# Small edits to a tuned kernel: bias groups, load order, tile order, zero fill, reciprocals

## The chip, the cores and the metric

The kernel runs on one core of a Trainium2 chip. The metric is the device time of one execution in microseconds (us), lower is better. TensorE is called PE in the rows, with PEld for its weight loads; VectorE is DVE, ScalarE is ACT, GpSimd is POOL, and SP is the engine that issues most DMAs.

## The reference

Attention with a relative bias made by a small network, then a routed expert layer, then a gated output layer. Cut to what matters here:

```python
scores = scale * np.matmul(q, k.transpose(0, 1, 3, 2))       # 2 batches, 8 heads, 576 rows, 64 wide
x = (psi_rel / psi_i)[..., None]                             # log1p|i-j| over log1p(max(i,1))
bias = np.maximum(x @ w1 + b1, 0.0) @ w2                     # hidden 32, one value for each head
scores = scores + bias.transpose(2, 0, 1)[None]
attn = np.exp(scores - np.max(scores, axis=-1, keepdims=True))
attn = attn / (np.sum(attn, axis=-1, keepdims=True) + 1e-09)
out = np.matmul(attn, v)
# then: each row goes to one of 8 experts (dropped rows stay zero), then a SwiGLU layer to [1152, 512]
```

## The kernel before

The order of every engine's instructions is written out by hand; an engine runs its own list in order, and a wait holds everything behind it on that engine.

**The bias phase** (`bias_phase`) makes the bias of all heads. For each of 36 groups `k` of 16 query rows, `hidden(k)` makes four tiles `r` of 128x576 (line 554 on DVE: multiply by a per-row slope `sl`, then max; or line 552 on ACT as a Relu). The fourth tile of a group goes to ACT when `k % 5` is in `ONA`, that is in 21 of the 36 groups. Sixteen small matmuls (line 558) contract them into the PSUM tile `pb`, the ACT tile first; there are two such tiles, and 12 buffers for `r`. `leave(k)` adds a constant `kap` on ACT (line 567) and stores the group to DRAM (`biasd`, line 568). On ACT the order is `r` of group k, then `leave` of group k-1. `kap` is copied by DVE (lines 541 and 542) from `pk`, a product that PE makes behind its 14 warming matmuls. From group 20 on, ACT and DVE also split the first head's queries and keys into a high and a low part.

SP first issues loads of `wb`, `cst`, `ptab` and the two halves of the table `ltab`, in this order, and later the stores and, after the last group, the last bias tiles of head 0 (lines 189 to 193).

**The attention phase** (`attn_phase`) walks through 72 tiles, nine for a head: four of batch 0, one that holds the last 64 rows of both batches (`t == 4`), four of batch 1. Step `u` issues, in this order: loads for the next head on SP (`load`, line 220, at `u % 9` of 0 and 5; `bias` at 1 to 5), the scores of tile u+1 (line 279), the exponential of tile u-1 (line 311), the transposes of tile u-2 (lines 331 and 334), the maximum of tile u (`bound`, line 294), the low part of tile u-3 (`low`, line 350), and a share of the queued products with V (`pv`, line 378) and folds (`folds`, line 400). `folds(h)` takes the sums of head h, adds 1e-9 and takes the reciprocal on DVE (lines 392 and 393), and scales the result `xh` (line 403), whose PSUM bank is single. By the written shares it runs at step 9h + 17.

A loaded head is split by POOL (lines 231 to 242): for each of two batches, five steps on the raw tile, of which there are two buffers. The scores of the next head wait for them (`K2`, line 235). At step 12 one DMA fills the whole output with zeros (line 435).

After attention come routing, the experts and the output layer, which are not touched.

Of the kernel before, what the change touches and what calls it, by code (L numbers as in the profile page):

```python
# [8 lines left out]
F32 = mybir.dt.float32  # L9
# [4 lines left out]
AF = mybir.ActivationFunctionType  # L14
ALU = mybir.AluOpType
# [3 lines left out]
B, H, S, D, C = 2, 8, 576, 64, 32  # L19
N, DM, E, FF, F2 = B * S, H * D, 8, 1024, 1536  # L20
# [3 lines left out]
NT = 9  # L24
# [19 lines left out]
ENGINES = {getattr(mybir.EngineType, e) for e in ("DVE", "Pool", "Activation", "PE", "SP")}  # L44


ONA = (1, 3, 4)
L0, L1 = 20, 2
STEPS1 = 4

LOADS = (0, 5)
SHARE, SHARE4 = 0.68, 0.0
LAST = (2.0, 2.0, 2.0, 2.0)
LATE = ((7, 0, 1), (7, 1, 0), (7, 1, 1))
# [84 lines left out]
def view(t, off, *dims):  # L139

    base = t[:]
    return bass.AP(tensor=base.tensor, offset=base.offset + off, ap=[list(base.ap[0])] + [list(d) for d in dims])
# [105 lines left out]
def attn_phase(tc, ctx, load, cst, bias, zeros, fold, lg, x_p, rows, ps):  # L248
    nc = tc.nc
    V, A = nc.vector, nc.scalar  # L250
# [3 lines left out]
    m_p = ctx.enter_context(tc.tile_pool(name="am", bufs=4))  # L254
    ident = cst[:, C_ID:C_ID + 128]
    load, qk, loads = load
    bias, head = bias
    seq = []
    for h in range(H):
        seq += [(h, 0, t) for t in range(4)] + [(h, -1, 4)] + [(h, 1, t) for t in range(4)]  # L260
    mid = {}
    sco, ex, tp, tt, sums, pt, ot = {}, {}, {}, {}, {}, {}, {}

    def batches(u):
        h, b, t = seq[u]
# [100 lines left out]
    def pv(h, b, n):  # L366

        if h not in ot:
            ot[h] = o_p.tile([128, N], F32, name="ot")
        o = ot[h]  # L370
        hi, lo = pt[h, b]
        W = qk[h, b][3]
        a, w = ((0, 256), (256, 320))[n]
        po = bank((h, b, n) in LATE)
        k = 0
        for kt in range(5):
            for src in ((hi, lo) if kt < 4 else (hi,)):
                nc.tensor.matmul(po[:, :w], W[:, kt], src[:, kt, a:a + w], start=k == 0, stop=k == 8)  # L378
                k += 1
                if k < 9:  # L380
                    yield w / 2400
        A.activation(o[:, b * 512 + a:b * 512 + a + 256], po[:, :256], AF.Copy)
        if w > 256:
            A.activation(o[:, 1024 + b * 64:1088 + b * 64], po[:, 256:w], AF.Copy)
        if n:
            del pt[h, b]
        yield 0

    def folds(h):
        o = ot.pop(h)  # L390
        rs = m_p.tile([128, NT], F32, name="rs")
        V.tensor_scalar(rs, sums[h], 1e-9, None, op0=ALU.add)
        V.reciprocal(rs, rs)
        xh = x_p.tile([128, NT * RW], F32, name="xh").rearrange("p (t c) -> p t c", t=NT)
        w = fold[:, h // 2, h % 2 * E:h % 2 * E + RW]
        x, g = (xh[:, :, E:], xh[:, :, :E]) if h % 2 == 0 else (xh[:, :, :D], xh[:, :, D:])
        for t0, tn in ((0, 5), (5, 4)):
            pf = bank(h == H - 1)[:, :5 * RW].rearrange("p (t c) -> p t c", c=RW)
            for t in range(t0, t0 + tn):
                nc.tensor.matmul(pf[:, t - t0], o[:, t * 128:(t + 1) * 128], w, start=True, stop=True)  # L400
                if t < t0 + tn - 1:
                    yield 0.12
            V.tensor_tensor(xh[:, t0:t0 + tn], pf[:, :tn], view(rs, t0, (1, tn), (0, RW)), op=ALU.mult)
            if t0:
                nc.sync.dma_start(
                    rows.rearrange("(t p) d -> p t d", p=128)[:, :, h * D:(h + 1) * D], x
                )
                if h == 0:
                    nc.gpsimd.tensor_copy(lg, g)
                else:  # L410
                    (V if h == H - 1 else nc.gpsimd).tensor_tensor(lg, lg, g, op=ALU.add)
            yield 0
# [1 line left out]
    nu = len(seq)  # L414

    work = []
    for h in range(H):
        work += [(9 * h + 6, pv(h, 0, 0))] + ([(0, folds(h - 1))] if h else [])
        work += [(9 * h + 9, pv(h, 0, 1)), (9 * h + 11, pv(h, 1, 0)), (9 * h + 13, pv(h, 1, 1))]
    work.append((0, folds(H - 1)))  # L420
    share = 0.0
# [1 line left out]
    while work:  # L423
        u += 1
        if u < nu:
            h, b, t = seq[u]
            if h + 1 < H and u % 9 in LOADS:
                b = LOADS.index(u % 9)
                loads.append(load(h + 1, b))
                qk[h + 1, b] = next(loads[-1])  # L430
            if h + 1 < H and 1 <= u % 9 <= NQ:
                bias(h + 1, u % 9 - 1)
            if u == 12:
                out, zi = zeros
                nc.sync.dma_start(out.rearrange("(t p) d -> p t d", p=128), view(zi, 0, (0, NT), (1, DM)))
        if u == 0:
            score(0)
        if u + 1 < nu:
            score(u + 1)
        if 0 <= u - 1 < nu:  # L440
            expo(u - 1, mx)
        if 0 <= u - 2 < nu:
            turn(u - 2)
        if u < nu:
            mx = bound(u)
        for n in (u - 5, u - 4):
            if n in tt:
                low_tail(n)
        if 0 <= u - 3 < nu:
            low(u - 3)  # L450

        first = u - 3 - (0 <= u - 3 < nu and seq[u - 3][2] in (1, 3))
        whole = 0 <= u - 3 < nu and seq[u - 3][2] not in (0, 2)
        if whole and u >= nu:
            turn_tail(first)
        share += SHARE if u < nu and seq[u][2] < 4 else SHARE4 if u < nu else LAST[min(u - nu, 3)]
        while work and work[0][0] <= u and share > 0:
            cost = next(work[0][1], None)
            if cost is None:
                work.pop(0)  # L460
            elif cost == 0:
                break
            else:
                share -= cost
        share = min(share, 0.3)
        if whole and u < nu:
            turn_tail(first)
        for n in range(2 if u > 3 else 3):
            if loads and next(loads[0], 0) == 0:
                loads.pop(0)  # L470
# [20 lines left out]
def bias_phase(tc, ctx, ins, cst, rt, biasd, bias, one, tids, ps, load, qk):  # L491
# [7 lines left out]
    r_p = ctx.enter_context(tc.tile_pool(name="bir", bufs=12))  # L499
    e_p = ctx.enter_context(tc.tile_pool(name="bie", bufs=6))  # L500
    wb = pool.tile([128, 2 + H], F32, name="wb")
    nc.sync.dma_start(wb, ins["wb"])
    nc.sync.dma_start(cst, ins["cst"])
    ptab = pool.tile([128, S // 4], F32, name="ptab")
    nc.sync.dma_start(ptab, ins["ptab"])
    ltab = pool.tile([128, 1148], F32, name="ltab")
    for j in (slice(508, 1148), slice(0, 508)):
        nc.sync.dma_start(ltab[:, j], ins["ltab"][:, j])
    loads = []
    for b in range(B):  # L510
        loads.append(load(0, b, "A", V))
# [12 lines left out]
    w1, b1 = wb[:, 0:1], wb[:, 1:2]  # L524
    nb = pool.tile([128, 1], F32, name="nb")
    V.tensor_scalar(nb, b1, -1.0, None, op0=ALU.mult)
    w2 = pool.tile([128, 4, H], F32, name="w2")
    V.scalar_tensor_tensor(
        w2, view(wb, 2, (0, 4), (1, H)), 8.0, view(cst, C_JJ, (1, 4), (0, H)), op0=ALU.mult, op1=ALU.mult
    )  # L530
    w2 = w2.rearrange("p a b -> p (a b)")
    sl = pool.tile([128, S // 4], F32, name="sl")
    V.tensor_scalar(sl, ptab, w1, None, op0=ALU.mult)
    strips = [slice(32 * g, 32 * g + 32) for g in range(4)]
    pk = ps.tile([128, 512], F32, name="pk", tag="P", bufs=1)
    for to in strips:
# [1 line left out]

    kap = pool.tile([128, 2], F32, name="kap")
    V.memset(kap[:, 1:], 0.0)  # L540
    V.tensor_copy(kap[:, :1], pk[:, :1])
    V.tensor_copy(kap[:96, 1:], pk[:96, :1])

    def hidden(k):
        r = []
        for g in range(4):
            i0 = 16 * k + 4 * g
            x = ltab[:, 572 - i0:572 - i0 + S]
            s = sl[:, i0 // 4:i0 // 4 + 1]
            r.append(r_p.tile([128, S], F32, name="r"))  # L550
            if g == 3 and k % 5 in ONA:
                A.activation(r[g], x, AF.Relu, scale=s, bias=b1)  # L552
            else:
                V.tensor_scalar(r[g], x, s, nb, op0=ALU.mult, op1=ALU.max)  # L554
        pb = ps.tile([128, 2, 512], F32, name="pb", tag="S")
        for c in range(2):
            for g in (3, 2, 0, 1):
                nc.tensor.matmul(  # L558
                    pb[strips[g], c, :288], w2, r[g][:, c * 288:(c + 1) * 288], start=True, stop=True,
                    skip_group_check=True,  # L560
                )
        return pb

    def leave(k, pb):
        o = e_p.tile([128, S], F32, name="be")
        n = int(k % 5 in ONA)
        A.activation(o.rearrange("p (c j) -> p c j", c=2), pb[:, :, :288], AF.Identity, bias=kap[:, n:n + 1])  # L567
        nc.sync.dma_start(biasd[k // 8][k % 8 * 16:k % 8 * 16 + 16].rearrange("i h j -> (i h) j"), o)

    pb = None  # L570
    for k in range(S // 16):
        last, pb = pb, hidden(k)
        if k:
            leave(k - 1, last)
        if k % 8 == 2 and k > 8:
            bias(0, k // 8 - 1)
        if k in (20, 21, 22):
            next(others, None)
        if k >= L0 and (k - L0) % L1 == 0:
            next(loads[0], None)  # L580
            if STEPS1 > (k - L0) // L1:
                next(loads[1], None)
# [773 lines left out]
```

## Time and profile before

| what | value |
|---|---|
| time of 3 runs | median 453.87 us (453.65 to 455.3) |
| profiled execution | 454.89 us, of which its span 453.0 us |
| bias phase | 0 to about 73 us |
| attention | about 73 to 228 us |
| routing, experts, output layer | about 228 to 453 us |
| busy share of the span | PE 88%, DVE 77%, ACT 61%, POOL 25% |
| mean granted TensorE clock | 0.971 |

The span is the time from the first to the last instruction of the profiled execution. Each stage has another limit, so a share of the whole span says little about a change to one stage.

### The profile page before, as it was taken

Reading aid. Unit: us, or ns where it says so; the run is one execution under the profiler, and the core shown is the slowest. Engines: PE = TensorE matmul, PEld = TensorE weight load, DVE = VectorE, ACT = ScalarE, POOL = GpSimd, SP = SyncE. Lnnn points to the kernel's source line nnn. Section 1 sums busy time; section 2 is a strip of 40 time slices with the busy share of each in tenths; the row PEclk is TensorE's granted clock in tenths of the full one; section 3 lists DMA queues with packets and bytes.
Section 4 is the critical chain, followed back from the end, with each engine's and each line's share of the span. In section 5 each row is a group of like instructions: output and inputs, shape, how many; then the busy total and the mean of one; then the engine's idle time right before and its main releaser. Section 6 shows DMA issues by size and latency. Waiting matters only on the chain.

```text
span 453.0 us, 8758 instructions
## 1 busy us (share of the span) xinstructions
PE 400.5 (88%) x3122; PEld 344.8 (76%) x3122; DVE 348.4 (77%) x745; ACT 274.6 (61%) x577; POOL 115.3 (25%) x109
## 2 busy tenths in 40 slices
PE   6776768799899999999987998997999999999993
PEld 4332225689799989889866888995988888888992
DVE  4999996789689998999784578874678888888441
ACT  2777767798689889789772448533443444444221
POOL 0000000695997876961002200010000000000003
PEclk9999899899899999999989799999999999999998
DMA  7455355889556749521188699986345444440003
GB/s 239 168 199 209 133 199 190 296 301 301 187 154 222 216 112 279 142 90 27 27 269 92 218 299 129 333 257 219 99 142 180 139 141 139 140 140 1 0 1 113
DMA packets 54081, 76.34 MB, mean 169 GB/s; under 512 B 16434, under 2 KB 35634, under 8 KB 54032
## 3 DMA queue, kind: packets, MB, share of 16 engines
q1 hardware_dynamic: 51616, 70.62, 49.0%
q0 software_dynamic: 800, 2.48, 3.1%
q10 hardware_dynamic: 1616, 2.62, 1.8%
q8 instruction: 26, 0.43, 0.4%
q14 instruction: 23, 0.19, 0.1%
HBM read 59.13 MB, written 16.59 MB: 167 GB/s over the span
## 4 chain that ended last, share of the span: by engine, by line
DVE 33%; PE 33%; ACT 15%; issue 9%; DMA 6%; POOL 3%; DVEq 0%; POOLq 0%; SPq 0%; ACTq 0%
PE pg L1229 9%; DVE r L554 7%; DMA xr<-rows,ri 4%; PE pb L558 4%; PE ph L978 4%; DVE swl L771 4%; ACT ex L311 4%; DVE wf L757 4%; ACT pth L334 3%; PE po L378 3%; DVE ptl L350 2%; PE py L992 2%; DVE sg L1237 2%; PE tp L331 2%; PE sc L279 2%
## 5 line engine op out<-in xcount | busy, mean ns | idle before, releaser
L558 PE MATMUL pb<-r,w 128*32 128x288 f32 x576 | 46.7, 437 | 18.8 <-DVE r L554 11.5
L294 DVE CUSTOM_DVE_ANT_0 ex<-sc,bias 128x576 f32<-128x576 f32 x72 | 53.9, 750 | 9.5 <-PE sc L279 3.0
L554 DVE TENSOR_SCALAR r<-ltab,sl,nb 128x576 f32<-128x576 f32 x123 | 60.6, 574 | 0.0
L231 POOL TENSOR_TENSOR QK<-raw,zero 128x640 fp32r<-128x640 f32 x28 | 34.5, 1254 | 99.3 <-DMA raw<-in_qkv 93.3
L311 ACT ACTIVATE ex<-ex,mx 128x576 f32<-128x576 f32 x72 | 55.8, 774 | 2.1 <-DVE mx L294 1.4
L558 PEld LDWEIGHTS pb<-r,w 128*32 128x32 f32 x576 | 18.9, 114 | 46.1 <-ACT r L552 15.8
L279 PE MATMUL sc<-QK 128*128 128x288 f32 x160 | 50.2, 330 | 3.1 <-DVE mx L294 2.2
L334 ACT ACTIVATE pth<-tp 128x512 fp32r<-128x512 f32 (+1 forms) x80 | 43.8, 553 | 12.3 <-PE tp L331 7.7
L350 DVE TENSOR_TENSOR ptl<-tp,pth 128x512 fp32r<-128x512 f32 (+1 forms) x80 | 50.0, 635 | 1.4 <-ACT pth L334 0.7
L1229 PE MATMUL pg<-x2h,swh 128*128 128x304 f32 x192 | 46.4, 308 | 4.9 <-DVE sg L1237 4.1
L279 PE MATMUL sc<-K,QK 128*128 128x288 f32 x160 | 46.0, 303 | 1.8 <-POOL K L235 1.8
L331 PE MATMUL tp<-cst,ex 128*128 128x128 f32 x288 | 45.1, 280 | 2.0 <-DVE ptl L350 1.2
L1229 PE MATMUL pg<-x2l,swh 128*128 128x304 f32 x192 | 43.9, 303 | 0.0
L1229 PE MATMUL pg<-x2h,swl 128*128 128x304 f32 x192 | 43.5, 301 | 0.0
L378 PE MATMUL po<-pth,W 128*128 128x256 f32 (+1 forms) x145 | 43.2, 320 | 0.0
L1261 POOL DMA_INDIRECT out<-ob,ids x5 | 4.9, 976 | 144.6 <-ACT ob L1258 143.7
L567 ACT ACTIVATE be<-pb,kap 128x576 f32<-128x576 f32 x36 | 26.6, 739 | 22.5 <-PE pb L558 13.3
L1229 PEld LDWEIGHTS pg<-x2h,swh 128*128 128x128 f32 x192 | 32.7, 188 | 9.7 <-DVE sg L1237 7.1
L1241 ACT ACTIVATE sh<-sg 128x608 fp32r<-128x608 f32 (+1 forms) x13 | 8.8, 674 | 51.1 <-DVE sg L1237 51.1
L331 PEld LDWEIGHTS tp<-cst,ex 128*128 128x128 f32 x288 | 33.8, 143 | 6.1 <-issue 2.5
L1237 DVE TENSOR_TENSOR sg<-pg,sg 128x304 f32<-128x304 f32 x48 | 20.7, 469 | 22.1 <-PE pg L1229 18.6
L279 PEld LDWEIGHTS sc<-QK 128*128 128x128 f32 x160 | 30.9, 193 | 5.0 <-DVE mx L294 3.1
(190 smaller groups left out, 1025.9 us busy)
## 6 DMA issues: line engine op xcount, KB each, us to landing
raw<-in_qkv SPq DMA_DIRECT2D x16, 800.0 KB, 6.5
biasd<-be SPq DMA_DIRECT2D x36, 288.0 KB, 2.2
wr<-in_ew SPq DMA_DIRECT2D x19, 512.0 KB, 6.8
w<-in_mwg SPq DMA_DIRECT2D x12, 512.0 KB, 3.7
w<-in_mwv SPq DMA_DIRECT2D x12, 512.0 KB, 4.7
w<-in_mwo SPq DMA_DIRECT2D x12, 512.0 KB, 5.8
bias<-biasd SPq DMA_DIRECT2D x16, 288.0 KB, 4.4
bias<-biasd SPq DMA_DIRECT2D x17, 256.0 KB, 4.4
```

The source lines that it names most:

```text
L231: P.tensor_tensor(QK[:, o:o + n], raw[:, o:o + n], view(zero, 0, (0, n)), op=ALU.add)
L279: nc.tensor.matmul(sc[:, c, :288], l, K[:, o + c * 288:o + (c + 1) * 288], start=n == 0, stop=n == len(lhs) - 1)
L294: V.tensor_tensor_reduce(e.rearrange("p (c j) -> p c j", c=2), sc[:, :, :288], head[h][:, t].rearrange("p (c j) -> p c j", c=2), scale=-0.125,
L311: A.activation(ex[u], ex[u], AF.Exp, bias=mx, scale=-1.0, accum_out=sums[h][:, col:col + 1])
L331: nc.tensor.transpose(x[:, kt], e[:, kt * 128:(kt + 1) * 128], ident)
L334: A.activation(hi[:, :4, c], x[:, :, o], AF.Copy)
L350: V.tensor_tensor(lo[:, :, c], x[:, :, o], hi[:, :4, c].bitcast(F32), op=ALU.subtract)
L378: nc.tensor.matmul(po[:, :w], W[:, kt], src[:, kt, a:a + w], start=k == 0, stop=k == 8)
L554: V.tensor_scalar(r[g], x, s, nb, op0=ALU.mult, op1=ALU.max)
L558: nc.tensor.matmul(pb[strips[g], c, :288], w2, r[g][:, c * 288:(c + 1) * 288], start=True, stop=True, skip_group_check=True,)
L1229: nc.tensor.matmul(g[:, :TB], w[:, a * 4 + kk], x[:, kk, c0 + b * TB:c0 + (b + 1) * TB], start=kk == 0 and i == 0, stop=kk == 3 and i == 2,)
L1237: V.tensor_tensor(sg[:, cs], g[:, :TB], sg[:, cs], op=ALU.mult)
```

## The change

`ONA` is now read with `k % 9`: 28 groups instead of 21 have their fourth tile on ACT. The two copies of `kap` go from DVE to ACT, behind the first group. SP loads the second half of `ltab` second, then `ptab`, `cst` and the first half. The tiles of head 0 are reordered: two of batch 0, two of batch 1, the others of batch 0, the shared tile, the others of batch 1; its products with V are queued in a matching order, and the load of head 1's second batch is issued at step 7 instead of 5. The zeros go out as nine DMAs, one at step 7 of each head and two in the last. The sum plus 1e-9 becomes a `tensor_tensor` with a tile of constants, and it and the reciprocal are issued at step 9h + 11 instead of with the fold.

```diff
-ONA = (1, 3, 4)
+ONA = (1, 2, 3, 5, 6, 7, 8)
-LOADS = (0, 5)
+LOADS0, LOADS = (0, 7), (0, 5)
...
-    for h in range(H):
+    seq = [(0, 0, 0), (0, 0, 1), (0, 1, 0), (0, 1, 1), (0, 0, 2), (0, 0, 3), (0, -1, 4), (0, 1, 2), (0, 1, 3)]
+    for h in range(1, H):
...
+    eps = m_p.tile([128, 1], F32, name="eps", bufs=1)
+    V.memset(eps, 1e-9)
...
+    def inv(h):
+        if h not in rsum:
+            rs = rsum[h] = m_p.tile([128, NT], F32, name="rs")
+            V.tensor_tensor(rs, sums[h], view(eps, 0, (0, NT)), op=ALU.add)
+            V.reciprocal(rs, rs)
+        return rsum[h]
...
-        rs = m_p.tile([128, NT], F32, name="rs")
-        V.tensor_scalar(rs, sums[h], 1e-9, None, op0=ALU.add)
-        V.reciprocal(rs, rs)
+        rs = inv(h)
...
+    work += [(6, pv(0, 0, 0)), (8, pv(0, 1, 0)), (11, pv(0, 0, 1)), (13, pv(0, 1, 1))]
...
-            if u == 12:
+            if u % 9 == 7:
                 out, zi = zeros
-                nc.sync.dma_start(out.rearrange("(t p) d -> p t d", p=128), view(zi, 0, (0, NT), (1, DM)))
+                for n in ((h,) if h + 1 < H else (h, NT - 1)):
+                    nc.sync.dma_start(out[n * 128:(n + 1) * 128], zi)
...
+        if u % 9 == 2 and u > 9:
+            inv(u // 9 - 1)
...
     nc.sync.dma_start(wb, ins["wb"])
+    nc.sync.dma_start(ltab[:, 508:], ins["ltab"][:, 508:])
+    nc.sync.dma_start(ptab, ins["ptab"])
     nc.sync.dma_start(cst, ins["cst"])
...
-    V.tensor_copy(kap[:, :1], pk[:, :1])
-    V.tensor_copy(kap[:96, 1:], pk[:96, :1])
...
-            if g == 3 and k % 5 in ONA:
+            if g == 3 and k % 9 in ONA:
...
-        if k:
+        if k == 0:
+            A.activation(kap[:, :1], pk[:, :1], AF.Copy)
+            A.activation(kap[:96, 1:], pk[:96, :1], AF.Copy)
+        else:
             leave(k - 1, last)
```

## Rows read from the trace of the kernel before

**Rows 1.** Stretch: us, busy PE, PEld, DVE, ACT, POOL, clock, DMA share, GB/s

```profile
20.00:40.00 20.00, 15.02 (x199) 6.39 (x194) 20.00 (x42) 13.84 (x20) 0.00 (x0) 1.00 0.52 197
...
116.00:120.00 4.00, 4.00 (x22) 3.99 (x23) 1.46 (x3) 0.84 (x2) 3.86 (x5) 0.61 0.55 176
```

**Rows 2.** Timeline of the start: start, duration, engine, line, idle before and releaser

```profile
2.14 0.91 SPq L508 DMA_DIRECT2D ltab<-in_ltab  x2
...
5.72 0.87 ACT L552 ACTIVATE r<-ltab,wb,sl 128x576 f32<-128x576 f32 x1 [3.48 <-DMA ltab<-in_ltab]
...
7.37 0.16 DVE L541 COPY kap<-pk 128x1 f32<-128x1 f32 x1 [3.49 <-PE pk L537]
...
7.51 12.81 DVE L554 TENSOR_SCALAR r<-ltab,sl,nb 128x576 f32<-128x576 f32 x26
```

**Rows 3.** Timeline of the bias phase: DVE, then one pair of groups

```profile
19.75 29.48 DVE L554 TENSOR_SCALAR r<-ltab,sl,nb 128x576 f32<-128x576 f32 x60
...
24.34 1.18 PE L558 MATMUL pb<-r,w 128*32 128x288 f32 x16 [0.34 <-ACT r L552]
25.71 0.74 ACT L567 ACTIVATE be<-pb,kap 128x576 f32<-128x576 f32 x1 [0.79 <-ACT be L567]
...
26.35 0.86 ACT L552 ACTIVATE r<-ltab,wb,sl 128x576 f32<-128x576 f32 x1
```

**Rows 4.** Chain that ended last, from the last bias group to head 1

```profile
72.86 0.75 ACT be L567
...
78.72 4.41 DMA raw<-in_qkv
...
87.45 1.55 POOL K L235
...
89.05 0.67 PE sc L279 x3
```

**Rows 5.** Timeline of DVE in head 0: its fourth and fifth tile

```profile
77.70 0.76 DVE L294 CUSTOM_DVE_ANT_0 ex<-sc,bias 128x576 f32<-128x576 f32 x1 [1.54 <-PE sc L279]
...
80.78 0.76 DVE L294 CUSTOM_DVE_ANT_0 ex<-sc,bias 128x576 f32<-128x576 f32 x1 [1.71 <-DMA bias<-biasd]
```

**Rows 6.** DMA issues: queue, count, KB each, median us to landing

```profile
raw<-in_qkv SPq DMA_DIRECT2D x16, 800.0 KB, 6.5
...
out<-zi SPq DMA_DIRECT2D x1, 2304.0 KB, 12.2
```

**Rows 7.** Timelines of SP, POOL and PE around head 2's second batch

```profile
98.01 0.33 SPq L220 DMA_DIRECT2D raw<-in_qkv  x1
...
110.01 2.47 POOL L231 TENSOR_TENSOR QK<-raw,zero 128x640 fp32r<-128x640 f32 x2 [4.66 <-DMA raw<-in_qkv]
...
115.77 0.61 PE L279 MATMUL sc<-K,QK 128*128 128x288 f32 x1 [1.22 <-POOL K L235]
```

**Rows 8.** Timeline of DVE: the first tile of heads 2, 3 and 4

```profile
108.42 0.75 DVE L294 CUSTOM_DVE_ANT_0 ex<-sc,bias 128x576 f32<-128x576 f32 x1
...
129.76 0.75 DVE L294 CUSTOM_DVE_ANT_0 ex<-sc,bias 128x576 f32<-128x576 f32 x1
...
147.49 0.75 DVE L294 CUSTOM_DVE_ANT_0 ex<-sc,bias 128x576 f32<-128x576 f32 x1
```

**Rows 9.** Instructions on tile rs, min/median/max in ns, and who waited

```profile
L392 DVE TENSOR_SCALAR rs<-sum x8: 163/410/1111, 107.5 to 224.5; 128x9 f32<-128x9 f32 x8
L393 DVE RECIPROCAL rs<-rs x8: 215/216/218, 107.7 to 224.7; 128x9 f32<-128x9 f32 x8
...
  PE po L400: 2.9, 5
```

**Rows 10.** Timelines of POOL and DVE: the longest addition, and an idle stretch

```profile
163.45 1.56 POOL L233 TENSOR_TENSOR QK<-raw,QK 64x640 fp32r<-64x640 f32 x1
...
163.93 1.11 DVE L392 TENSOR_SCALAR rs<-sum 128x9 f32<-128x9 f32 x1
...
153.71 0.59 DVE L356 TENSOR_TENSOR pth<-tt,pth 64x128 fp32r<-64x128 f32 x2 [0.52 <-ACT pth L345]
```

More of the change, by code (lines that the diff above doesn't have):

```diff
@@ L257, in attn_phase @@
     bias, head = bias
-    seq = []
-    for h in range(H):
+    seq = [(0, 0, 0), (0, 0, 1), (0, 1, 0), (0, 1, 1), (0, 0, 2), (0, 0, 3), (0, -1, 4), (0, 1, 2), (0, 1, 3)]
+    for h in range(1, H):
         seq += [(h, 0, t) for t in range(4)] + [(h, -1, 4)] + [(h, 1, t) for t in range(4)]
     mid = {}
-    sco, ex, tp, tt, sums, pt, ot = {}, {}, {}, {}, {}, {}, {}
+    sco, ex, tp, tt, sums, pt, ot, rsum = {}, {}, {}, {}, {}, {}, {}, {}
+    eps = m_p.tile([128, 1], F32, name="eps", bufs=1)
+    V.memset(eps, 1e-9)
     def batches(u):
@@ L416, in attn_phase @@
     work = []
-    for h in range(H):
-        work += [(9 * h + 6, pv(h, 0, 0))] + ([(0, folds(h - 1))] if h else [])
+    work += [(6, pv(0, 0, 0)), (8, pv(0, 1, 0)), (11, pv(0, 0, 1)), (13, pv(0, 1, 1))]
+    for h in range(1, H):
+        work += [(9 * h + 6, pv(h, 0, 0)), (0, folds(h - 1))]
         work += [(9 * h + 9, pv(h, 0, 1)), (9 * h + 11, pv(h, 1, 0)), (9 * h + 13, pv(h, 1, 1))]
@@ L426, in attn_phase @@
             h, b, t = seq[u]
-            if h + 1 < H and u % 9 in LOADS:
-                b = LOADS.index(u % 9)
+            at = LOADS if h else LOADS0
+            if h + 1 < H and u % 9 in at:
+                b = at.index(u % 9)
                 loads.append(load(h + 1, b))
@@ L501, in bias_phase @@
     wb = pool.tile([128, 2 + H], F32, name="wb")
+    ltab = pool.tile([128, 1148], F32, name="ltab")
+    ptab = pool.tile([128, S // 4], F32, name="ptab")
     nc.sync.dma_start(wb, ins["wb"])
+    nc.sync.dma_start(ltab[:, 508:], ins["ltab"][:, 508:])
+    nc.sync.dma_start(ptab, ins["ptab"])
     nc.sync.dma_start(cst, ins["cst"])
[L504 to L508, printed above, removed]
+    nc.sync.dma_start(ltab[:, :508], ins["ltab"][:, :508])
     loads = []
@@ L526, in bias_phase @@
     V.tensor_scalar(nb, b1, -1.0, None, op0=ALU.mult)
+    sl = pool.tile([128, S // 4], F32, name="sl")
+    V.tensor_scalar(sl, ptab, w1, None, op0=ALU.mult)
     w2 = pool.tile([128, 4, H], F32, name="w2")
@@ L531, in bias_phase @@
     w2 = w2.rearrange("p a b -> p (a b)")
-    sl = pool.tile([128, S // 4], F32, name="sl")
-    V.tensor_scalar(sl, ptab, w1, None, op0=ALU.mult)
     strips = [slice(32 * g, 32 * g + 32) for g in range(4)]
@@ L565, in leave @@
         o = e_p.tile([128, S], F32, name="be")
-        n = int(k % 5 in ONA)
+        n = int(k % 9 in ONA)
         A.activation(o.rearrange("p (c j) -> p c j", c=2), pb[:, :, :288], AF.Identity, bias=kap[:, n:n + 1])
```

## The prediction

> **What bounds the kernel now.** I read the stages first, as busy time by stretch, then the timelines and the chain of waits inside the two stages that the diff touches. Everything behind attention is untouched, so what counts is by how much attention ends sooner.
>
> In the bias phase DVE is busy 20.00 of 20 us while ACT is busy 13.84 and PE 15.02 [rows 1]: DVE sets the pace. Its 60 tiles take 29.48 us, 0.491 us each [rows 3]. It starts late: the second half of the table has landed at 5.7 us, because ACT starts a tile at 5.72 when that load releases it, but DVE's first tile starts at 7.51. The copies of `kap` stand ahead of it in DVE's list, and they wait 3.49 us for PE's `pk`, which is behind the warming matmuls [rows 2].
>
> In head 0 DVE idles 1.54 us before its fourth tile, which the view puts down to PE though its bias tile also comes last in the queue, and 1.71 us before its fifth, for a bias load [rows 5]. The chain of waits, however, does not run through DVE there: it goes from the raw load for head 1 (78.72, 4.41 us) through POOL's splitting to `K2` (87.45, 1.55 us) and to the first scores of head 1 at 89.05 [rows 4].
>
> In head 2 the same happens with more waiting. POOL idles 4.66 us until a raw load lands, and PE then waits for the `K2` made from it until 115.77 [rows 7]. In the four us that follow the granted clock is 0.61, so PE was mostly at 1.2 GHz instead of 2.4 [rows 1]. From the first tile of head 2 to that of head 3 it takes 21.34 us, from head 3 to head 4 17.73 [rows 8].
>
> In the later heads the wait is around the fold. The addition of 1e-9 to nine sums takes 163 ns at best and 1111 at worst, the reciprocal always about 216 [rows 9]. The worst case shows why: the addition starts at 163.93, while POOL's instruction of 163.45 runs, and ends at 165.04 with it at 165.01 [rows 10]. PE waits 2.9 us in all, in five heads, for the scaled result behind this pair before it can refill the single bank [rows 9].
>
> **The change part by part.**
>
> *Start.* The table's half moves from the fourth load to the second, two issues earlier; two issues last 0.91 us [rows 2], so it lands at about 4.8 instead of 5.7. `ptab` and `cst` now come behind it, and the slopes and weights that DVE makes from them stand ahead of the first tile. DVE can start no sooner than 4.8 and hardly later than the 5.7 at which everything has landed today; I take 5.4. The `kap` copies leave its list. Gain 7.51 - 5.4 = 2.1 us, bounds 1.8 and 2.7. The copies cost ACT two instructions of one element; it was waiting for the table then, and its next tile must only be ready when DVE has made seven. If ACT were late, that tile would hold PE, not DVE, which has 12 buffers.
>
> *Seven more tiles on ACT.* DVE loses 28 - 21 = 7 tiles of 0.491: 3.4 us. ACT gains 7 of 0.86 [rows 3], 6.0 us of some 68, where it is busy about 0.69 of the time [rows 1]; on average it fits. Locally it is close. In a run of groups that all have a tile on ACT, the loop of two groups goes from PE's start (24.34) to `leave` (25.71) to the next ACT tile (26.35) to its end, 27.21: 2.87 us [rows 3]. DVE needs six tiles, 2.95 us, in that time. So DVE still sets the pace, by a margin of 0.08. The splits that ACT also does from group 20 on make it late, which the 12 buffers of `r` (three groups) cover, and each group without an ACT tile gives 0.49 us back. I take the whole 3.4 us; the lower bound is none.
>
> *Head 0's order and the later load.* The fourth tile of batch 0 and the shared tile are asked for two steps later, which removes the idle 1.54 + 1.71 us [rows 5]. But nothing in the diff moves the raw load of head 1: it stands on SP behind the last bias tiles of head 0, which need the last group's store. From `leave` of the last group (72.86) to the load's issue (78.72) and on to head 1's first scores (89.05) is 16.2 us [rows 4], and I expect the same distance. PE comes to head 1's scores about 3 us sooner and waits there instead. Value taken: 0, upper bound 3.25 us. The products with V that are queued for step 8 stand behind those scores on PE, so they do not fill the wait. A wait of some 4 us in one piece also does what it did in head 2: the clock of 0.61 over four us loses 4 x 0.39 = 1.6 us of PE work [rows 1]. Cost taken 1.6, bounds 0 and 2. The load at step 7 is issued behind five bias loads instead of three; POOL takes it up only when the first batch is split, at least 7 us after that one landed, and the median load lands in 6.5 us [rows 6], so it should be in time.
>
> *Zeros in nine.* The one transfer is 2304 KB and lands in 12.2 us [rows 6]; the raw load issued behind it at 98.01 held POOL until 110.01 [rows 7], 12.0 us against the median 6.5. With 256 KB there instead, it should land by about 104.5, before POOL has finished the load ahead of it at 110.01 - 4.66 = 105.35. PE's wait and the slow clock go. Gain 21.34 - 17.73 = 3.6 us [rows 8]; at least the 1.22 us of the last wait [rows 7]. The other parts go out in heads that have no such queue, ahead of loads that POOL takes up much later.
>
> *Reciprocals.* Addition and reciprocal leave the place between `low` and the scaling. The chain there goes on to PE, which idles 2.9 us in sum [rows 9]; behind that PE's own list (scores and transposes) comes next, so I take 2.9 and not the pairs' whole length; bounds 0 and 2.9. At step 9h + 11 DVE gets 0.16 + 0.22 = 0.4 us [rows 9], and shortly behind that place it idles 0.52 us for ACT's tail [rows 10]. Cost 0 if the new addition doesn't wait. No row shows an addition of two SBUF tiles on DVE while POOL works. Between 0.16 and the longest POOL instruction near it, 1.56, I take the first for the sum, since the reciprocals, one SBUF input and no faster mode to be seen, never waited; the other end is a rival. The Trainium skill (SBUF — State Buffer, section "SBUF: two separate sides") speaks against this edit: an instruction of VectorE with two SBUF inputs takes the port pair shared with GpSimd, just as one in a 2-port mode does, and is blocked for the whole of a GpSimd instruction that reads SBUF. Row 163.93 agrees for the old form; by the rule the new form would wait as well, and only its place would help.
>
> **Sum.** -2.1 - 3.4 + 0 + 1.6 - 3.6 - 2.9 = -10.4 us. The profiled execution took 454.89 us, so 444.5; it lies 1.0 above the median of the runs, so 443.5.
>
> **The rivals.**
>
> 1. *The addition still waits, for the POOL instruction that runs.* For it: the pattern of row 163.93. Half of an instruction of 1.56 is 0.8; with 0.4 of work and 0.5 of idle time, 0.7 us shows in each of six heads (POOL has nothing left in the last), 4 us if nothing else hides it; ACT's exponentials run behind DVE there, so I count half. 445.5.
> 2. *The gain in head 0 is kept*, because the raw load lands sooner or head 1 catches up. Against it: the chain [rows 4]. Then 3.25 us come and the 1.6 of the clock don't go: 438.6.
> 3. *ACT sets the bias phase's pace.* For it: the margin of 0.08 us. If a group with an ACT tile lasts 0.12 us longer than DVE's 1.47, 28 of them eat the 3.4 us: 446.9.
> 4. *The wait in head 2 stays*, because the bias loads alone delay the raw load: 447.1.
> 5. *Slower: the addition loses the port to more than one POOL instruction.* POOL's instructions follow each other closely at step 9h + 11. The place is DVE's list in six heads. A wait of w shows as w + 0.4 - 0.5; the 10.4 us are used up from 1.8 us on, that is once a second instruction gets in. With two, 3.1 us, it is 3.0 x 6 = 18 us: 461.5. Against it: the longest addition ended with the first instruction, in none of eight did it take longer than 1.11 us [rows 9, 10].
>
> **How the numbers follow.** Forecast 0.45, rival 1 0.25, rival 2 0.10, rival 3 0.12, rival 4 0.05, rival 5 0.03. The forecast's own range, from the bounds of the start, the clock and the fold, is 441 to 446. To leave out no more than 2 in 10, it must reach to rivals 1, 3 and 4 and half-way to rival 2: 439.5 to 448. About 0.5%, 2.3 us, is what a measurement of this kernel can tell from no change; all but rival 5 are faster by more, save for mishaps together: faster 0.95, same 0.02, slower 0.03.
>
> **What would show it.** DVE's first tile near 5.4 us; DVE still without idle time to group 35 and the last `leave` near 67.4 (72.86 - 5.5); the same 16.2 us from there to head 1's first scores, with one PE wait of some 4 us for POOL and a lower clock behind it; no wait for `K2` in head 2; the scaling right behind `low`, heads of about 17.4 us; additions of 0.16 us at step 2 of each head. The prediction is wrong if DVE idles for buffers of `r`, if the new additions take a microsecond and show in the heads' length, or if head 1 starts sooner after the last bias group.

## The result, and the profile after

The changed kernel takes 447.71 us (median of 4 runs, 446.49 to 449.84) against 453.76 before: ratio 0.9867, 95% interval 0.9822 to 0.9912. It is 6.05 us faster where 10.4 were forecast; the time lies inside the predicted range, near its slow end. The profiled execution took 446.49 us (span 444.6) against 454.89 (span 453.0), 8.4 us less. So of the 4.2 us by which the median misses 443.5, 2.0 stand in the profile (446.5 instead of 444.5); the other 2.2 are how each profiled execution lies to its own median, 1.0 above before, as the prediction took it, and 1.2 below after. Of all runs one (of e5, 452.12 us at a clock of 0.961) was slow, over 1.5% above the fastest of its kernel, and is left out of e5's median.

The shift is followed best by DVE's `ex`, the first vector instruction on each tile of scores. Starts in us, from the timelines of DVE (`e1` and so on are the experiments below; the last column goes to the end of the span). The other tiles in the rows: `sc` scores, `tp` and `tt` transposes, `pth` and `ptl` the high and low part of the transposed exponentials, `po` the products with V (P V), `be` a finished bias group, `xr` rows gathered for an expert.

| kernel | first `ex` | head 1 | head 2 | head 3 | last `ex` | from there to the end |
|---|---|---|---|---|---|---|
| before | 73.63 | 90.41 | 108.42 | 129.76 | 217.12 | 235.9 |
| changed | 67.58 | 88.35 | 107.99 | 125.20 | 209.52 | 235.1 |
| e1 changed, again | 67.94 | 89.60 | 109.24 | 126.45 | 210.59 | 235.4 |
| e2 old order | 67.77 | 86.48 | 106.26 | 124.18 | 208.62 | 235.3 |
| e3 early load | 67.86 | 84.73 | 106.37 | 123.87 | 208.42 | 237.7 |
| e4 both | 67.84 | 88.30 | 105.99 | 123.64 | 208.06 | 237.1 |
| e5 no second load | 67.44 | 89.54 | 110.53 | 127.73 | 211.91 | 235.4 |
| e6 both loads early | 67.46 | 84.23 | 105.21 | 122.41 | 206.90 | 234.9 |
| e7 the same, old order | 67.46 | 88.05 | 105.75 | 122.95 | 207.33 | 236.7 |
| e8 zeros in one | 67.88 | 90.37 | 111.35 | 128.56 | 212.72 | 235.1 |
| e9 P V sooner | 68.48 | 88.88 | 106.29 | 123.51 | 207.41 | 234.3 |
| e10 combined | 67.42 | 83.17 | 100.84 | 118.05 | 202.35 | 236.0 |
| e11 old reciprocals | 67.78 | 89.47 | 110.76 | 128.87 | 214.75 | 235.3 |
| e12 old bias share | 70.97 | 91.54 | 111.22 | 128.43 | 212.80 | 235.8 |

The change arrives at the first `ex` with 6.05 us in hand, at head 2 with 0.43 left, at head 3 with 4.56, at the last tile with 7.60. Two stretches need explaining: what head 0 and head 1 lose, and whether head 2's gain is that of the zeros.

*Start and bias phase.* The timeline of the changed kernel's start, and the 76 tiles of DVE in the middle of the phase:

```profile
2.62 0.44 SPq L521 DMA_DIRECT2D ltab<-in_ltab  x1
...
4.99 0.58 DVE L565 TENSOR_SCALAR r<-ltab,sl,nb 128x576 f32<-128x576 f32 x1
...
7.19 0.17 ACT L585 ACTIVATE kap<-pk 128x1 f32<-128x1 f32 x1 [4.95 <-PE pk L550]
...
7.44 37.31 DVE L565 TENSOR_SCALAR r<-ltab,sl,nb 128x576 f32<-128x576 f32 x76
```

DVE's first tile starts at 4.99 instead of 7.51 [rows 2]: 2.5 us. The `kap` copies wait on ACT now, and DVE loses nothing by it. The tiles still take 37.31 / 76 = 0.491 us each, as in [rows 3], so the other 3.5 us are the seven tiles fewer.

*Head 0 to head 1.* Busy time by stretch of the changed kernel (PE, PEld, DVE, ACT, POOL, clock, DMA share, GB/s), then its chain of waits:

```profile
80.00:84.00 4.00, 0.40 (x1) 0.19 (x1) 1.60 (x4) 1.33 (x4) 3.84 (x4) 1.00 1.06 283
84.00:88.00 4.00, 3.40 (x15) 3.39 (x16) 0.00 (x0) 0.66 (x2) 3.79 (x5) 0.57 0.53 168
88.00:92.00 4.00, 3.52 (x25) 2.77 (x23) 3.53 (x11) 3.59 (x11) 3.84 (x4) 1.00 0.99 381
```

```profile
65.61 4.86 DMA bias<-biasd
70.48 1.58 DMA bias<-biasd
...
73.78 4.93 DMA raw<-in_qkv
...
83.01 1.54 POOL K L235
...
84.59 1.09 PE sc L282 x3
85.69 0.85 PE tp L334 x4
86.54 1.66 PE po L381 x8
88.20 0.12 PE tt L344
88.35 0.63 DVE ex L297
```

The piece of the chain that is shown begins with the bias tile that is loaded twice: the second half of the second load goes out when the first load has landed (65.61 + 4.86). Three more issues on SP stand between it and the raw load. The last `leave` starts at 66.81, head 1's first scores at 84.59: 17.8 us, not the 16.2 of [rows 4]. PE is busy 0.40 of 4 us before that, and the clock behind it is 0.57: most of those four us at 1.2 GHz. Then head 1's first `ex` doesn't follow the scores, as it did before; four transposes, eight P V matmuls and a `tt` stand between, and it needs the `tt` to free its buffer. Inside head 0 the two waits of [rows 5] are gone, as forecast (timeline of DVE):

```profile
70.32 0.76 DVE L297 CUSTOM_DVE_ANT_0 ex<-sc,bias 128x576 f32<-128x576 f32 x1 [0.22 <-PE sc L282]
...
73.29 0.75 DVE L297 CUSTOM_DVE_ANT_0 ex<-sc,bias 128x576 f32<-128x576 f32 x1
...
88.35 0.76 DVE L297 CUSTOM_DVE_ANT_0 ex<-sc,bias 128x576 f32<-128x576 f32 x1 [6.75 <-PE tt L344]
```

*Inside head 1* stands a wait that the trace before doesn't have (timelines of PE, ACT and DVE):

```profile
92.81 0.39 PE L381 MATMUL po<-pth,W 128*128 128x320 f32 x1
...
95.59 0.40 PE L381 MATMUL po<-pth,W 128*128 128x320 f32 x1
...
96.02 0.60 ACT L337 ACTIVATE pth<-tp 128x512 fp32r<-128x512 f32 x1 [3.13 <-PE po L381]
...
97.09 0.59 DVE L359 TENSOR_TENSOR pth<-tt,pth 64x128 fp32r<-64x128 f32 x2 [1.95 <-ACT pth L348]
...
98.53 0.63 PE L334 MATMUL tp<-cst,ex 128*128 128x128 f32 x4 [2.02 <-DVE ptl L353]
```

ACT stands 3.13 us until the last matmul of `pv(0, 0, 1)` has read the `pth` buffer, of which each batch has one; DVE and PE then wait for ACT in turn. Eight of the nine matmuls are done by 94.23. The ninth, for which the step's share did not suffice, comes at 95.59, behind the scores of the next tiles.

*Head 2 and later.* The DMA issues, POOL's second batch of head 2, and DVE's first tiles of heads 2, 3 and 4, which answer to [rows 6 to 8]:

```profile
raw<-in_qkv SPq DMA_DIRECT2D x16, 800.0 KB, 5.7
...
out<-zi SPq DMA_DIRECT2D x9, 256.0 KB, 7.2
```

```profile
100.91 2.47 POOL L231 TENSOR_TENSOR QK<-raw,zero 128x640 fp32r<-128x640 f32 x2
...
107.99 0.75 DVE L297 CUSTOM_DVE_ANT_0 ex<-sc,bias 128x576 f32<-128x576 f32 x1
...
125.20 0.75 DVE L297 CUSTOM_DVE_ANT_0 ex<-sc,bias 128x576 f32<-128x576 f32 x1
...
143.11 0.75 DVE L297 CUSTOM_DVE_ANT_0 ex<-sc,bias 128x576 f32<-128x576 f32 x1
```

POOL takes up this batch without idle time, and head 2 lasts 17.21 us instead of 21.34. POOL's next wait for a raw load, 4.43 us until 121.95 for head 3's second batch, holds nothing up. From head 3's first tile to the last one it takes 84.32 us against 87.36, 3.0 less. The view of the tile `rs`, and POOL beside the first addition:

```profile
L395 DVE TENSOR_TENSOR rs<-sum,eps x8: 158/181/1190, 92.9 to 215.0; 128x9 f32<-128x9 f32 x8
L396 DVE RECIPROCAL rs<-rs x8: 215/216/217, 93.7 to 215.2; 128x9 f32<-128x9 f32 x8
...
  PE po L408: 1.6, 6
```

```profile
92.78 0.87 POOL L242 TENSOR_TENSOR W<-raw,W 128x320 fp32r<-128x320 f32 x1
...
92.87 0.81 DVE L395 TENSOR_TENSOR rs<-sum,eps 128x9 f32<-128x9 f32 x1
```

The new addition waits for POOL's instruction just as the old one did [rows 10]: it ends at 93.68, POOL's at 93.65. In this view 1.6 us stand under PE's `po` as time that DVE waited for it; the 2.9 us that PE waited for the scaled result [rows 9] are gone. The longest addition stands in head 3 (timelines of POOL and DVE):

```profile
129.58 2.46 POOL L231 TENSOR_TENSOR QK<-raw,zero 128x640 fp32r<-128x640 f32 x2
...
129.67 1.19 DVE L395 TENSOR_TENSOR rs<-sum,eps 128x9 f32<-128x9 f32 x1
```

What an addition costs can be read from the length of the heads. At the old place (heads 3 to 6 before and in e11) a head lasts 17.27 us and the whole addition on top, within 0.02 us in all eight. At the new place (heads 3 to 6 of the changed kernel and of the other eleven experiments, 48 heads) it lasts 17.20 to 17.31 us with additions of up to 0.65 us, 17.37 to 17.61 with 0.74 to 0.96, and 17.68 to 17.91 with 1.05 to 1.25. So the new place hides about 0.6 us of an addition, and what is longer shows.

### The profile page after: what moved, and what is told of

It reads as the page before. It is cut to its first block, busy times and chain, and to the rows that moved or that the text cites. A ratio compares the mean times of both kernels' runs of the same rounds, so it can differ in the third digit from the quotient of the medians.

```text
span 444.6 us, 8757 instructions
## 1 busy us (share of the span) xinstructions
PE 396.1 (89%) x3122; PEld 342.5 (77%) x3122; DVE 343.1 (77%) x737; ACT 279.1 (63%) x586; POOL 115.5 (26%) x109
## 4 chain that ended last, share of the span: by engine, by line
PE 44%; DVE 21%; ACT 10%; issue 6%; DMA 5%; POOL 2%; SPq 0%; DVEq 0%; POOLq 0%; ACTq 0%
PE pg L1243 9%; PE tp L334 6%; PE po L381 5%; PE sc L282 5%; PE ph L992 5%; PE py L1006 4%; DVE swl L785 4%; DVE wf L771 4%; PE po L408 3%; DMA bias<-biasd 2%; DVE sg L1251 2%; ACT pth L337 2%; PE pb L569 2%; DMA xr<-rows,ri 2%; ACT ex L314 2%
## 5 line engine op out<-in xcount | busy, mean ns | idle before, releaser
L569 PE MATMUL pb<-r,w 128*32 128x288 f32 x576 | 45.2, 424 | 14.4 <-ACT r L563 9.4
L565 DVE TENSOR_SCALAR r<-ltab,sl,nb 128x576 f32<-128x576 f32 x116 | 57.2, 570 | 0.0
L282 PE MATMUL sc<-QK 128*128 128x288 f32 x160 | 49.1, 324 | 3.6 <-POOL QK L233 3.1
L282 PE MATMUL sc<-K,QK 128*128 128x288 f32 x160 | 45.0, 297 | 1.2 <-POOL K L235 1.2
L334 PEld LDWEIGHTS tp<-cst,ex 128*128 128x128 f32 x288 | 32.8, 142 | 11.0 <-ACT ex L314 4.6
L381 PE MATMUL po<-ptl,W 128*128 128x256 f32 (+1 forms) x116 | 33.4, 308 | 0.0
```

The lines of the kernel that those rows point to most:

```text
L282: nc.tensor.matmul(sc[:, c, :288], l, K[:, o + c * 288:o + (c + 1) * 288], start=n == 0, stop=n == len(lhs) - 1)
L334: nc.tensor.transpose(x[:, kt], e[:, kt * 128:(kt + 1) * 128], ident)
L569: nc.tensor.matmul(pb[strips[g], c, :288], w2, r[g][:, c * 288:(c + 1) * 288], start=True, stop=True, skip_group_check=True,)
```

## The experiments

Edits are against the changed kernel unless said otherwise. Medians are of 4 runs, of 3 for e5, 6 for e10 and 10 for e11 and e12. Runs e1 to e4, e5 to e8 and e9 to e12 were each measured together, every series on another chip; the kernel before had medians of 453.70, 454.13 and 453.08 beside them. The same changed kernel gave 447.71 and 448.74, so less than about 1.5 us between two medians settles nothing, and between two series the kernel before alone differs by up to 1.05. A timeline is of one execution: in e12 of the fastest, 2.4 us below its median.

**e1, e2: the order of head 0.** e1 is the changed kernel unedited. e2:

```
-LOADS0, LOADS = (0, 7), (0, 5)
+LOADS0, LOADS = (0, 5), (0, 5)
-    seq = [(0, 0, 0), (0, 0, 1), (0, 1, 0), ...
-    for h in range(1, H):
+    seq = []
+    for h in range(H):
-    work += [..., (8, pv(0, 1, 0)), (11, pv(0, 0, 1)), ...
+    work += [..., (9, pv(0, 0, 1)), (11, pv(0, 1, 0)), ...
```

> The changed kernel once more, as the foot of the 2x2 design that the next three runs make with it. All theories: 447 to 448 us, first scores of head 1 ready 17.7 us after the last `be` of the bias phase ends (trace before: 16.2), first `ex` of head 1 near 88.3.

> The changed kernel with head 0's tiles, its P V order and its load slots as in the kernel before; all else stays changed. Theory A (the new order costs time: head 1's first scores hang on a raw load behind the last bias tiles in either order, and in the new order the pair buffer of the first `ex` of head 1 and eight P V matmuls at the low clock collect behind them): 3 to 4.5 us faster than the changed kernel, 443.3 to 444.7. Theory B (order makes no difference, the lost 5.6 us are the slower clock and the longer DMA chain): within 1 us of the changed kernel. Theory C (the new order gains its 3.25 us of waits, and something else lost 8.9): 3 us slower, about 451.

Measured: e1 448.74 us (ratio to before 0.9887, 0.9827 to 0.9948), e2 444.79 (0.9782, 0.9721 to 0.9844). e1 misses its expectation: head 1's first `ex` is at 89.60, not 88.3, since POOL starts 6.69 us behind the raw load's issue, in the first run 5.08. By the medians the reorder costs 4.0 us instead of bringing any, theory A's size; the two profiled executions lie 2.05 apart. Head 1's first `ex` comes 3.1 us sooner in the old order, although POOL's `K2` is hardly earlier there (timelines of PE and DVE in e2; in e1 the scores go on at 85.99):

```profile
85.77 0.40 PE L282 MATMUL sc<-K,QK 128*128 128x288 f32 x1 [1.22 <-POOL K L235]
...
86.48 0.76 DVE L297 CUSTOM_DVE_ANT_0 ex<-sc,bias 128x576 f32<-128x576 f32 x1 [1.40 <-PE sc L282]
```

From there to the `ex` it takes 0.71 us, in e1 3.61: what collects behind the scores is the difference. Head 1 itself is not shorter in the old order (19.78 us against 19.64). And from the first `ex` to head 2 e2 takes 38.49 us, 3.7 more than before. Of that 2.6 is the longer way to head 1's first scores, 18.00 us behind the first `ex` instead of 15.42; e1 has 18.05, so the order has no part in it.

**e3, e4: head 1's first raw load inside the bias phase**, in the new and in the old order:

```
+        if k == 33:
+            loads.append(load(1, 0))
+            qk[1, 0] = next(loads[-1])
-            if h + 1 < H and u % 9 in at:
+            if h + 1 < H and u % 9 in at and (h + 1, at.index(u % 9)) not in qk:
```

> The changed kernel with one load moved: head 1's first raw load goes out inside the bias phase (behind group 33's bias tile instead of behind the last one and the duplicate load of bias(0, 3)). Theory A (the pin is the raw load's place on SP, so that K2 of head 1 comes 17.7 us after the last bias tile): the 3.11 and 1.21 us waits of PE on POOL go, the clock stays up, the first `ex` of head 1 comes 5 to 6 us sooner: 441 to 443 us. Theory B (the clock after the bias phase or ACT sets the pace, whatever the load): within 1 us of the changed kernel. POOL's start is what to look at: at 78.86 in the changed kernel.

> Both edits: head 0 in the old order, and head 1's first raw load inside the bias phase. Theory A: the load no longer pins, but the old order waits for late bias tiles (1.54 and 1.71 us in the trace before), so it gains little over the old order alone: 442 to 444 us, 1 to 3 us slower than the new order with the early load. Rival: the order is worth nothing once the load is early, and the two runs with the early load agree within 1 us.

Measured: e3 447.28 us, e4 445.15. Theory A was half right. In e3 head 1 does start 4.9 us sooner than in e1, but head 1 then lasts 21.64 us instead of 19.64, and the time misses the 441 to 443. The timelines of e3, POOL and ACT:

```profile
87.07 2.46 POOL L231 TENSOR_TENSOR QK<-raw,zero 128x640 fp32r<-128x640 f32 x2 [10.08 <-DMA raw<-in_qkv]
...
94.40 0.60 ACT L337 ACTIVATE pth<-tp 128x512 fp32r<-128x512 f32 x1 [5.13 <-PE po L381]
```

The second raw load is late now (POOL idles 10.08 us for it), and ACT's wait for the P V product is still there, longer than before. e4 misses both of its expectations: it was to be 1 to 3 us slower than e3 or equal to it, and is 2.1 faster. With one load early the old order is still the better one. e3 and e4 also lose some 2 us behind attention; see the end.

**e5, e6, e7: the rest of SP's queue.** e5 leaves out one of two identical loads of bias tile 3. e6 is e3 with that, and with the second raw load in step 1; e7 is e6 in the old order.

```
     leave(S // 16 - 1, pb)
-    bias(0, 3)
     bias(0, 4)
-LOADS0, LOADS = (0, 7), (0, 5)     # e6, e7 only
+LOADS0, LOADS = (0, 1), (0, 5)
```

> The changed kernel without the second, identical load of head 0's bias tile 3 that stands behind the last bias group on SP (the first goes out at group 34). Theory A (the path from the last `be` to head 1's first scores runs through SP, and the second load's wait for the first one's landing stands in it): the raw load goes out 1 to 2 us sooner, the first `ex` of head 1 comes 1 to 2 us sooner, 446 to 447.5 us. Theory B (SP has slack behind the bias phase): within 0.5 us of the changed kernel's 448.7.

> As e3_early_raw, and without the second load of bias tile 3, and with head 1's second raw load in step 1 instead of step 7. The theory after e3 (moving only the first raw load hands the pin to the second one: POOL stood idle for 10.08 us until 87.07, and ACT and DVE waited 5.13 and 4.45 us for the P V product and its transposes behind it): POOL's second batch of head 1 begins by 82, the waits of head 1 go, the first `ex` of head 2 comes 3 us sooner than in e3 (106.4), 442 to 444.5 us. Rival (the slow clock after the bias phase or the bias loads are the limit): not under 446.

> As e6_early_both with head 0's tiles, P V order in the old order. If the new order is worth its 3.25 us once nothing pins head 1: 2 to 3.5 us slower than e6_early_both. If it is worth nothing: within 1 us of it. Against e2_old_order (444.8): 1 to 3 us faster, if the raw loads pin there too.

Measured: e5 449.38 us (0.9856, 0.9760 to 0.9951), e6 443.29 (0.9762, 0.9704 to 0.9819), e7 445.59. In e5 my theory fell; its timeline of SP and its chain:

```profile
71.31 0.53 SPq L189 DMA_DIRECT2D bias<-biasd  x1
...
73.14 0.43 SPq L220 DMA_DIRECT2D raw<-in_qkv  x1
```

```profile
67.43 2.76 DMA biasd<-be
...
73.14 6.62 DMA raw<-in_qkv
```

Without the second load the queue waits at the next one, for tile 4, which needs the store of the last bias group; the raw load goes out 6.48 us after the last `leave` (66.66), in e1 6.39 (in the first run 6.97), and POOL starts 6.77 us behind its issue, in e1 6.69: nothing is gained. e6 met its expectation in time, 443.29, and in POOL, which takes up the second batch at 81.29; PE no longer waits for POOL at head 1. But a wait inside head 1 stays, and head 2 comes 1.2 us sooner than in e3, not 3. With both loads early the new order beats the old one by 2.3 us (e6, e7); with the loads late it lost 4.0. e7 was also to be 1 to 3 us faster than e2 and is 0.8 slower: to the old order the early loads bring nothing. Two waits stay in e6, both on ACT:

```profile
73.68 0.60 ACT L337 ACTIVATE pth<-tp 128x512 fp32r<-128x512 f32 x1 [3.46 <-DMA biasd<-be]
...
91.90 0.60 ACT L337 ACTIVATE pth<-tp 128x512 fp32r<-128x512 f32 x1 [3.13 <-PE po L381]
```

**e8: the zeros in one transfer**, in step 12 as before:

```
-            if u % 9 == 7:
+            if u == 12:
                 out, zi = zeros
-                for n in ((h,) if h + 1 < H else (h, NT - 1)):
-                    nc.sync.dma_start(out[n * 128:(n + 1) * 128], zi)
+                nc.sync.dma_start(out.rearrange("(t p) d -> p t d", p=128), view(zi, 0, (0, NT), (1, DM)))
```

> The changed kernel with the zeros of the output in one transfer in step 12, as before, instead of nine parts. The prediction's term: 3.6 us slower than the changed kernel, 452 us, with a wait for the raw load of head 2 in place (in the trace before raw at 98.01 waited and PE stood 1.22 us at 115.77). Rival (the head 2 wait came from the kernel's other timing, not from the zeros): within 1 us of the changed kernel.

Measured: 448.28 us (0.9861, 0.9800 to 0.9922), no slower than the changed kernel: the rival. The timelines of POOL and DVE:

```profile
107.21 2.47 POOL L231 TENSOR_TENSOR QK<-raw,zero 128x640 fp32r<-128x640 f32 x2 [4.57 <-DMA raw<-in_qkv]
...
111.35 0.75 DVE L297 CUSTOM_DVE_ANT_0 ex<-sc,bias 128x576 f32<-128x576 f32 x1
...
128.56 0.75 DVE L297 CUSTOM_DVE_ANT_0 ex<-sc,bias 128x576 f32<-128x576 f32 x1
```

POOL idles 4.57 us behind the one transfer, as before (4.66 [rows 7]), but head 2 lasts 17.21 us all the same. Before, POOL took this batch up 1.6 us after head 2's first `ex`; here 4.1 us ahead of it. The delay of head 1 covers the wait.

**e9: the second product sooner.**

```
-    work += [..., (8, pv(0, 1, 0)), (11, pv(0, 0, 1)), (13, pv(0, 1, 1))]
+    work += [..., (8, pv(0, 1, 0)), (10, pv(0, 0, 1)), (13, pv(0, 1, 1))]
+        share += 0.25 * (u == 10)
         while work and work[0][0] <= u and share > 0:
```

> The changed kernel with one part of the reorder undone: head 0's second product for its first batch, pv(0, 0, 1), from step 11 back to step 10 (9 before the change), with enough of the step's share that all nine matmuls go out in it. Theory (the one buffer of `pth` for that batch is held by this product, so head 1's first turn waits on ACT, 3.12 us in e1, with DVE's 1.97 and PE's 2.02 behind it): those three waits fall to under 1 us, head 1 takes 18 us instead of 19.6 to 21, and the kernel 1.5 to 2.5 us less than the changed kernel's 448.7. Rival (the buffer only hides the wait for POOL's second batch): head 1 unchanged, same time within 1 us.

Measured: 445.25 us (0.9806, 0.9748 to 0.9864), 3.5 less than e1; head 1 lasts 17.41 us. The timelines of e9, PE's first and last matmul of the product and ACT's next write to that buffer:

```profile
91.71 0.39 PE L381 MATMUL po<-pth,W 128*128 128x320 f32 x1
...
92.97 0.31 PE L381 MATMUL po<-pth,W 128*128 128x320 f32 x1
...
94.46 0.59 ACT L337 ACTIVATE pth<-tp 128x512 fp32r<-128x512 f32 x1
```

That wait of ACT is gone, and head 1 is 2.2 us shorter (17.41 instead of 19.64), the size expected. Another 1.3 us lie in head 0, where POOL starts 5.22 us behind the raw load's issue instead of 6.69; that the edit did this is not shown. The edit moves the product one step and gives it a larger share; which of the two was needed was not separated.

**e10: combined.** e6 and e9, with the first raw load at `k == 31`.

> e6_early_both with the edit of e9_pv_soon, and the first raw load at group 31 instead of 33 (in e6 the 800 KB of that load ran beside the last `be` stores, whose memory the first `pth` tile takes over: ACT stood 3.46 us at 73.68). If both waits were on the path: 2 + 2.5 us off e6's 443.3, 438.5 to 441. If the clock or the bias tiles take their place: 442 to 443.5.

Measured: 440.57 us (0.9715, 0.9667 to 0.9763), as expected, and faster than both kernels. The two edits were not tried one by one on e6. POOL and DVE in its timelines:

```profile
65.28 2.46 POOL L231 TENSOR_TENSOR QK<-raw,zero 128x640 fp32r<-128x640 f32 x2 [63.97 <-DMA raw<-in_qkv]
...
83.17 0.76 DVE L297 CUSTOM_DVE_ANT_0 ex<-sc,bias 128x576 f32<-128x576 f32 x1 [0.59 <-PE tt L344]
```

Head 0 lasts 15.75 us and head 1 17.67. From the first `ex` to head 3 it takes 50.6 us, in the changed kernel 57.6, before 56.1.

**e11, e12: the two other parts undone.**

```
+            V.tensor_scalar(rs, sums[h], 1e-9, None, op0=ALU.add)   # e11, in place of tensor_tensor
-        if u % 9 == 2 and u > 9:
-            inv(u // 9 - 1)
...
-ONA = (1, 2, 3, 5, 6, 7, 8)     # e12
+ONA = (1, 3, 4)                 # and k % 5 for k % 9, twice
```

> The changed kernel with the reciprocals as before the change: a tensor_scalar addition at the fold's place in the work list. The prediction's term: 2.9 us slower than the changed kernel, with heads 3 to 7 each about 1 us longer (18.3 instead of 17.2 to 17.4). Rival (the later heads got faster because head 2's traffic left, not by the reciprocals): heads 3 to 7 unchanged, same time within 1 us.

> The changed kernel with ACT's old share of the bias phase (three groups in five instead of seven in nine). The prediction's term: 3.4 us later at the first `ex` (71.3 instead of 67.9) and, if what stands behind it moves as a block, 3.4 us slower. Rival (the end of the bias phase is not what the attention phase waits for: the stores, loads and POOL are): first `ex` 3.4 us later, but first `ex` of head 2 under 1.5 us later, total under 2 us slower.

Measured: e11 452.47 us (0.9988, 0.9956 to 1.0020), e12 452.77 (0.9983, 0.9948 to 1.0018): 3.7 and 4.0 slower than e1. In e11 heads 2 to 7 take 104.0 us, in e1 101.4: 2.6 of it is the reciprocals. Heads 3 to 6 are not each about 1 us longer, as expected, but as long as 17.27 us and their addition (17.43 to 18.46). The additions of heads 2 to 6 take 3.0 us there and show in full; in e1 only one shows, with 0.5 us. The edit undoes form and place together, but the old form waits no longer than the new one (up to 1.19 us each), so the gain is the place's. The rest lies in head 1 (21.29), where e5 and e8, which keep the new place, lose about as much (20.99, 20.98). In e12 the first `ex` is 3.0 us later, head 2's 2.0 and the last 2.2, between term and rival; only the median is 4.0 later. The raw load goes out 5.89 us behind the last `leave`, as before (5.86). First `ex` of e12:

```profile
70.97 0.76 DVE L297 CUSTOM_DVE_ANT_0 ex<-sc,bias 128x576 f32<-128x576 f32 x1 [2.20 <-ACT be L578]
```

## Why the prediction was right in sign and short in size

The sum had -10.4 us; the profiled executions differ by 8.4, the medians by 6.05. That the time still lies in the range is luck: the forecast's own part of it ended at 446, and it was stretched to 448 for rivals 1, 3 and 4, of which only rival 1 came in part, with 0.7 us.

- **Start, -2.1:** right, -2.5 (first DVE tile at 4.99, expected 5.4).
- **Seven tiles on ACT, -3.4:** right, -3.5 at the first `ex`; DVE kept the pace, so rival 3 is out. e12 gives 4.0 by the medians, 2.6 by the profiled executions.
- **Head 0's order, 0, and clock, +1.6:** this is the step that failed. From the first `ex` to head 2 the changed kernel takes 40.41 us instead of 34.79: 5.6 lost where 1.6 was booked. The pin itself was seen rightly: PE stood for `K2`, and the clock fell to 0.57. Three things were not. The distance from the last `leave` grew from 16.2 to 17.8 us: the raw load left 6.97 us behind it (before 5.86) and took 4.93 (4.41). The first `ex` of head 1 had to wait for a buffer that a `tt` behind eight P V matmuls frees: 3.76 us from the scores to the `ex`, before 1.36. And `pv(0, 0, 1)`, moved from step 9 to 11, was costed at nothing, though it holds the one `pth` buffer that head 1 writes first: 3.13 us of ACT. The first of the three is not the order's: e2, in the old order, has it too. In e12, with ACT's old share, the raw load's issue is back at 5.89 us, which speaks for the faster bias phase; why the load then lands later is open. By the medians e2 prices the new order at +4.0 and e9 the move of that product at +3.5, but the second is no part of the first: e2 gains its time in head 0 (18.71 us against 21.66) and none in head 1, e9 2.2 us in head 1.
- **Zeros, -3.6:** the size came true (-4.1 in head 2), the reason didn't hold. The split does end POOL's wait, but e8, without it, has the same head 2, because head 1's delay lets POOL get ahead. Rival 4 is out: POOL doesn't idle for head 2's second batch in the changed kernel. Whether the split earns its term where head 1 is not late was not tried. The two terms were not independent: a delay ahead of a stall pays for the stall. Over the three heads together the change lost 1.5 us (57.6 against 56.1) where the sum had -2.0.
- **Reciprocals, -2.9:** right in size, -3.0 from head 3 to the last tile. Putting the old place back (e11) costs 1.7 in that stretch and 2.6 over heads 2 to 7; what it costs hangs on how the additions meet POOL, 2.1 us in heads 3 to 6 of e11 and 3.6 before. The addition of 0.16 us was wrong: it took up to 1.19, each long one ending with a POOL instruction. That is rival 1's mechanism. By the Trainium skill (SBUF — State Buffer, section "SBUF: two separate sides") two SBUF inputs block DVE against a GpSimd operation that reads SBUF as well. Rows 92.78 and 92.87 agree: the addition ends 0.03 us behind POOL's instruction. The price of rival 1 shows once: heads 4 to 6 last 17.2 to 17.3 us, with additions of up to 0.62, and head 3, with the 1.19, lasts 17.9, 0.7 longer. That is the price rival 1 gave for a head, in one of six instead of all. The prediction's own sign of being wrong, an addition of a microsecond that shows in a head's length, came there. The reason was wrong too: the term was taken from PE's 2.9 us of waiting, while at the old place the head's length takes the whole addition. The place made the gain, not the operation. Rival 5 is out: its 3.1 us never came, the longest addition of all runs took 1.27 us (e2).
- **Behind attention, 0:** the changed kernel takes 0.8 us less there (235.1 instead of 235.9) in code that nothing touched.
- One by one, from the start's row and the medians against e1 (start, ACT's share, order, zeros, reciprocals): -2.5 - 4.0 + 4.0 + 0.5 - 3.7 = -5.7, against -5.0 for e1 beside its own before and -6.05 in the first measurement. The intervals of the ratios are 0.3 to 0.6% wide to either side, 1.4 to 2.8 us, so this agreement proves no single term.

Rival 2 (head 0's gain kept) was out in this kernel; e10 shows what it would have needed: both raw loads early and the product in time. Whether e10's head 2 still needs the zeros split was not tried.

## What to carry to other kernels

When tiles are reordered, go through every later user of each single buffer that the moved steps hold: here a product moved by two steps held ACT for 3.1 us in the next head, about as much as the reorder was to save, and the head was 2.2 us shorter once it came sooner. A gain in front of a point that something else pins turns into a wait; move the pin first (the load), then the second pin behind it, and only then does the order pay. Two terms that lie one behind the other on the same chain, a delay and a stall, must not be added. An operation whose wait can't be avoided is put where its engine has time to spare: here the same addition showed in full at one place and only beyond 0.6 us at the other.

## What was unexpected

- A load brought forward can hold up the stores beside it: with 800 KB at group 33, ACT stood 3.46 us at 73.68 in e6 for a `be` store, whose memory the first `pth` tile seems to take over. Two groups sooner (e10) that wait is gone.
- Code behind attention that nothing touched took 237.7 and 237.1 us in e3 and e4, 235.1 to 235.4 in the changed kernel, 236.0 in e10. What differs is the arrival of the gathered rows: DVE idles 3.65 us for the second part's transfer in e4, 1.96 in e1. PE's transposes of two parts in e1 and one in e4, from their timelines:

```profile
240.60 0.55 PE L937 MATMUL etp<-cst,xr 96*128 96x96 f32 x4 [1.89 <-DVE xr L916]
243.13 0.90 PE L937 MATMUL etp<-cst,xr 96*128 96x96 f32 x4 [0.79 <-ACT xr L918]
```

```profile
239.77 0.90 PE L940 MATMUL etp<-cst,xr 96*128 96x96 f32 x4 [3.59 <-DVE xr L919]
```

  Why the gathered rows come later there is open; no run was made for it.
